# One more expert by seven products, an attention stage moved, and loads in another order: a fused attention and expert kernel

## The chip, the cores and the metric

The kernel runs on one core of a Trainium2 chip. The metric is the device time of one execution in microseconds (us). The kernel before has a median of 362.59 us in 3 runs (362.31 to 362.99). The engines are named as in the profile: PE is TensorE's matmuls, PEld its weight loads, DVE is VectorE, ACT ScalarE, POOL GpSimd and SP SyncE, which mostly issues transfers.

## The reference

Two parts follow each other. The first is attention in blocks: the keys and values of 4 batches of 8 heads (768 positions, 64 wide) are mixed block by block with a matrix that five rounds of exponential and normalisation make from `sort_net`; each of the 8 blocks of queries then attends to one block of 96 mixed keys and values. The second is a mixture of 4 experts on the 3072 resulting rows of 512 values.

```python
k_sorted = np.einsum('bhij,bhjcd->bhicd', P, k_b).reshape(B, H, S, D)
v_sorted = np.einsum('bhij,bhjcd->bhicd', P, v_b).reshape(B, H, S, D)
...
scores = scale * np.matmul(q_b, k_sb.transpose(0, 1, 2, 4, 3))
attn = softmax(scores)                       # written out in the reference
attn_out = np.matmul(attn, v_sb)
...
p = domain_probs / (domain_probs.sum(-1, keepdims=True) + 1e-09)
for e in range(E):                           # x: 3072 x 512, w1[e]: 512 x 1024, w2[e]: 1024 x 512
    h = np.maximum(x @ w1[e], 0.0)
    out += p[:, e:e + 1] * (h @ w2[e])
```

## The kernel before

The rows of a batch are worked on in three chunks of 256. The 12 chunks are numbered g = 0 to 11, and g = 5 (`G0`) is the third chunk of batch 1, counting batches from 0. The attention of a batch is spread in small stages over the expert chunks of earlier batches: each chunk calls `slot()` at fixed places, and a plan says which stages run there. An entry `(2, 0, st_x, 3, 2)` means: chunk 2, slot 0, stage `st_x` for batch 3, pair of heads 2. The program keeps its order on every engine.

The first layer (x times w1) of early chunks is ordinary: for each expert 8 blocks of output, 4 matmuls of 256 columns each, evicted by VectorE from two buffers of PSUM.

```python
def chunk_first(b, c, es, first, slot):
    ...
    for e in es:
        for g in range(2):
            ps = psm([P, 4, 2 * P], F32, ...)
            for f in range(4):
                for kc in range(NKC):                      # NKC = 4
                    nc.tensor.matmul(ps[:, f, :], w1sb[e][:, kc, ...], xT[:, kc, ds(2 * c * P, 2 * P)], ...)
            nc.vector.scalar_tensor_tensor(out=Hb[...], in0=ps[:], scalar=0.0, op0=ALU.max, in1=pb[...], op1=ALU.mult)
            ...                                            # block sums of the expert before
            slot()
```

From G0 on the first layer goes by seven products of half-size blocks in place of eight (a Strassen-like scheme). It needs four sums of weight blocks for each expert (`input_sums`: s1, s3, n2, s4) and four sums of token blocks (`token_sums`). Each product is 8 matmuls of 128 columns. X, Z and Q are PSUM banks of 512 columns; ScalarE copies Z to X so that both go on accumulating:

```python
def seven(g, e):
    ...
    def p1():
        product(Z, "a11", "b11", True)
        nc.scalar.copy(X, Z)
    def p5():
        product(Q, "s1", "t1", True)
    def p6():
        product(X, "n2", "n2")
        nc.scalar.copy(u2, X)
    def p2():
        product(Z, "a12", "b21")
        finish(0, 0, Z)                # VectorE: relu, times the expert's weight
    def p7():
        product(X, "s3", "t3")
        nc.scalar.copy(u3, X)
        tt(t22, Q, u3, ALU.add)
    def p4(): ...                      # X, then finish(1, 0, X)
    def p3(): ...                      # Q, then t12 = Q + u2
```

At G0 expert 0 is still ordinary, and the seven products start with expert 1. `last_banks(n)` closes a PSUM pool, takes four banks (X, Z, two Q) in its place and opens X with one matmul of 512 columns:

```python
def last_chunk(g, slot=None):
    lead = int(g == G0)
    if lead:
        chunk_first(b, c, [0], 0, slot)
        last_banks(0)
        last_tmp(g)
        prs = {1: seven(g, 1)}
        prs[1][1](); prs[1][5](); seven(g, 2)[5](); prs[1][2](); prs[1][6]()
        input_sums(0, 0, True)
        input_sums(0, 1, True)
        last_banks(1)
    else:
        last["e0"][2]()
        prs = {0: last["e0"]}
    ...
    for e in range(1 + lead, E):
        now, prev = prs[e], prs[e - 1]
        now[1]()
        prev[7]()
        ...
        now[2]()
        now[6]()
        prev[22](); prev[4](); prev[3]()
```

In later chunks expert 0's p1 and p5 run in the chunk before, between output products (`last_begin`), and its p6 inside the b22 product. The sums of weight blocks are made ahead. For experts 0 and 1 VectorE adds; for 2 and 3 ScalarE copies a block and a transfer of GpSimd's queue adds to it:

```python
def input_sums(e, n, vector=False):
    ...
    if vector:
        nc.vector.tensor_tensor(a[dst], a[y], a[x], ...)
    else:
        nc.scalar.mul(a[dst], a[x], sign)
        nc.gpsimd.dma_start(a[dst], a[y], accum_op=ALU.add)

PLAN_A = [    # chunk, slot, expert, which sum, on VectorE
    (1, 8, 1, 0, True), (1, 8, 1, 1, True), (1, 8, 1, 2, True), (1, 10, 1, 3, True),
    (1, 8, 2, 0), (1, 8, 2, 1), (1, 9, 3, 0), (1, 10, 3, 1), (1, 11, 2, 2), (1, 12, 3, 2), (1, 13, 2, 3),
    (2, 0, 3, 3),
]
```

The second layer of a chunk is seven products too, of 16 matmuls of 256 columns. The end of the chunk ahead of G0:

```python
    two = [psm([P, 2, 512], F32, ...) for n in range(2)]
    bankA, bankB, bankC, bankQ = [two[n // 2][:, n % 2, 0:DH] for n in range(4)]
    times(bankA, blk(0, 0), "b11", es)
    ...
    times(bankA, blk(0, 1), "t3", es, False)
    tt(ob2, bankA, p5[:], ALU.add)
    tt(ob1, bankA, ob1, ALU.add)
    store(1, ob)
    slot()                                     # slot 13: st_a(3, 2)
    times(bankQ, blk(1, 0), "b22", es, False)
    tt(oa2, bankQ, u2[:], ALU.add)
    slot()                                     # slot 14: st_a(3, 3), the last attention stage
    store(0, oa)
```

`st_a` is probabilities times values: two groups of 8 matmuls into the two buffers of a PSUM pool, each evicted by a reciprocal and a product on VectorE. The end of the last chunk of all:

```python
    product(bankQ, sm(0), "t1")
    nc.scalar.copy(p5[:], bankQ)
    product(bankA, sm(1), "t2", False)
    nc.scalar.copy(u2[:], bankA)
    ...
    product(bankQ, blk(1, 0), "b22", False, range(2))
    product(bankA, blk(0, 1), "t3", False)
    tt(ob2, bankA, p5[:], ALU.add)
    tt(ob1, bankA, ob1, ALU.add)
    nc.sync.dma_start(o[:, 2 * c + 1, :], ob[:])
    product(bankQ, blk(1, 0), "b22", False, range(2, E))
    tt(oa2, bankQ, u2[:], ALU.add)
    nc.sync.dma_start(o[:, 2 * c, DH:Dm], oa2)
```

Early in the program GpSimd issues the loads of batch 1 behind those of six weight matrices of 1 MB:

```python
for qd in range(2):
    for nm in ("v", "k"):
        load_natural(1, nm, qd)
    if qd == 0:
        load_queries(1, range(2))
```

`st_q` transposes a pair of query heads by a transfer of SyncE's queue (slot 7 of chunk 0 for the first pair of batch 1), `st_v` and `st_k` mix values and keys (slots 9 to 11), `st_s` makes scores (slot 0 of chunk 1).

The softmax here doesn't subtract the row's maximum and nothing guards it: scores larger than these inputs give would overflow.

## Time and profile before

| what | value |
|---|---|
| median time | 362.59 us |
| span of the profiled run | 362.4 us |
| instructions | 10776 |
| PE busy | 98% of the span |
| PEld busy | 87% |
| DVE busy | 76% |
| ACT busy | 48% |
| POOL busy | 37% |
| mean transfer rate | 112 GB/s |

Busy times are sums over the whole span; what a single change is worth is read from the stage that it touches. A timeline line gives start and duration in us, then the engine, the source line of the kernel before, the operation, what it writes and reads with partitions and elements, how many instructions are merged, and in brackets how long the engine was idle before and who released it. The duration of a merged group of matmuls includes the modelled run-out of the last one, so that the starts of neighbouring groups are the better measure. A line of the list of waits gives the total in us, how often, and the longest.

### The profile page before, as it was taken

Reading aid. Unit: us, or ns where it says so; the run is one execution under the profiler, and the core shown is the slowest. Engines: PE = TensorE matmul, PEld = TensorE weight load, DVE = VectorE, ACT = ScalarE, POOL = GpSimd, SP = SyncE. Lnnn points to the kernel's source line nnn. Section 1 sums busy time; section 2 is a strip of 40 time slices with the busy share of each in tenths; the row PEclk is TensorE's granted clock in tenths of the full one; section 3 lists DMA queues with packets and bytes.
Section 4 is the critical chain, followed back from the end, with each engine's and each line's share of the span. In section 5 each row is a group of like instructions: output and inputs, shape, how many; then the busy total and the mean of one; then the engine's idle time right before and its main releaser. Section 6 shows DMA issues by size and latency. Waiting matters only on the chain.

```text
span 362.4 us, 10776 instructions
## 1 busy us (share of the span) xinstructions
PE 354.0 (98%) x4589; PEld 315.0 (87%) x4589; DVE 276.8 (76%) x560; ACT 173.6 (48%) x305; POOL 134.1 (37%) x148
## 2 busy tenths in 40 slices
PE   8899999989999999999999999999999999999996
PEld 8785857778888888988889999999999998999995
DVE  5654898769788777868978978867779679587794
ACT  2664330451434355377938257165283481561740
POOL 8872010736022330000626318137055082180470
PEclk9999999999999999999999999999999999999999
DMA  7999999999999999935995210210401201102101
GB/s 99 207 207 231 209 209 202 194 187 194 214 116 142 203 127 173 165 70 69 179 192 88 60 60 2 60 60 3 89 32 50 70 3 58 62 2 63 56 15 46
DMA packets 71676, 40.47 MB, mean 112 GB/s; under 512 B 40518, under 2 KB 66380, under 8 KB 71628
## 3 DMA queue, kind: packets, MB, share of 16 engines
q0 software_dynamic: 36560, 19.93, 41.6%
q1 hardware_dynamic: 35068, 19.85, 27.4%
q8 instruction: 36, 0.59, 0.7%
q14 instruction: 12, 0.10, 0.1%
HBM read 42.00 MB, written 6.34 MB: 133 GB/s over the span
## 4 chain that ended last, share of the span: by engine, by line
PE 75%; DMA 18%; DVE 3%; SPq 1%; ACT 1%; issue 1%; POOL 0%; DVEq 0%; ACTq 0%; POOLq 0%
PE ps_Q L1141 24%; PE ps_h L768 13%; PE ps_p L753 10%; PE ps_X L1038 10%; DMA arena<-in_q_dram 8%; PE ps_Q L1038 7%; PE ps_Z L1038 7%; DMA w<-in_moe_w_dram 6%; DMA vs<-arena 2%; DMA qT<-arena 2%; PE ps_a L441 2%; PE ps_s L406 1%; SPq L368 1%; PE ps_v L354 1%; PE ps_k L387 1%
## 5 line engine op out<-in xcount | busy, mean ns | idle before, releaser
L1051 POOL TENSOR_TENSOR Hb<-tmp,pb 128x512 f16<-128x512 f32 x40 | 50.8, 1277 | 84.3 <-ACT tmp L1050 83.1
L768 PE MATMUL ps_h<-xT,w 128*128 128x256 f16 x576 | 67.8, 273 | 0.0
L768 PEld LDWEIGHTS <-w 128*128 128x128 f16 x576 | 55.1, 98 | 7.4
L774 DVE SCALAR_TENSOR_TENSOR Hb<-ps_h,pb 128x1024 f16<-128x1024 f32 x36 | 44.0, 1223 | 19.8 <-PE ps_h L768 19.6
L1141 PEld LDWEIGHTS <-Hb 128*128 128x128 f16 x560 | 53.4, 98 | 5.6
L1038 PEld LDWEIGHTS <-w 128*128 128x128 f16 x864 | 52.4, 98 | 1.0
L1141 PE MATMUL ps_Q<-w,Hb 128*128 128x256 f16 x336 | 43.4, 273 | 0.0
L1038 PEld LDWEIGHTS <-arena 128*128 128x128 f16 x552 | 33.4, 98 | 0.3 <-issue 0.2
L413 ACT ACTIVATE ET<-ps_s 96x768 f16<-96x768 f32 x24 | 18.1, 802 | 28.4 <-PE ps_s L406 28.1
L121 POOL DMA_DIRECT2D arena<-in_q_dram x24 | 19.9, 836 | 26.9 <-DMA qT<-arena 16.6
L1038 PE MATMUL ps_X<-kT,arena 128*128 128x128 f16 x384 | 29.3, 219 | 0.1
L1074 DVE TENSOR_TENSOR tmp<-ps_Q,tmp 128x512 f32<-128x512 f32 x26 | 18.0, 692 | 14.6 <-ACT tmp L1073 10.4
L1058 ACT COPY ps_X<-ps_Z 128x512 f32<-128x512 f32 x27 | 15.4, 570 | 28.3 <-PE ps_Z L1038 27.9
L396 ACT CAST kT<-ps_k 64x384 f16<-64x384 f32 x48 | 22.7, 473 | 12.8 <-PE ps_k L387 11.8
L739 DVE TENSOR_TENSOR Sb<-Hb 128x512 f16<-128x512 f16 x45 | 26.3, 609 | 0.9 <-POOL Hb L1051 0.8
L1141 PE MATMUL ps_Q<-T,Hb 128*128 128x256 f16 x224 | 26.7, 273 | 0.0
L1050 ACT ACTIVATE tmp<-tmp 128x512 f32<-128x512 f32 x40 | 25.4, 634 | 1.2 <-DVE tmp L1074 1.0
L753 PEld LDWEIGHTS <-Hb 128*128 128x128 f16 x232 | 21.9, 98 | 3.0
L1141 PEld LDWEIGHTS <-Sb 128*128 128x128 f16 x224 | 21.9, 98 | 2.5
L1065 ACT COPY tmp<-ps_X 128x512 f32<-128x512 f32 x26 | 15.2, 586 | 13.2 <-PE ps_X L1038 13.2
L1051 POOL TENSOR_TENSOR Hb<-tmp7x,pb 128x512 f16<-128x512 f32 x14 | 19.0, 1356 | 5.7 <-ACT tmp7x L1050 5.7
L1044 DVE SCALAR_TENSOR_TENSOR Hb<-ps_X,pb 128x512 f16<-128x512 f32 x27 | 18.5, 684 | 2.7 <-PE ps_X L1038 2.7
(205 smaller groups left out, 652.7 us busy)
## 6 DMA issues: line engine op xcount, KB each, us to landing
w<-in_moe_w_dram POOLq DMA_DIRECT2D x7, 1024.0 KB, 27.4
pb<-p_dram SPq DMA_DIRECT2D x12, 512.0 KB, 5.4
arena<-in_k_dram POOLq DMA_DIRECT2D x8, 384.0 KB, 8.8
arena<-in_v_dram POOLq DMA_DIRECT2D x8, 384.0 KB, 8.9
vs<-arena SPq DMA_DIRECT2D x36, 66.0 KB, 5.7
arena<-in_q_dram POOLq DMA_DIRECT2D x24, 96.0 KB, 7.3
out_dram<-ob SPq DMA_DIRECT2D x9, 256.0 KB, 2.0
out_dram<-oa SPq DMA_DIRECT2D x8, 256.0 KB, 2.3
```

What stands on the lines that cost most here:

```text
L121: nc.gpsimd.dma_start(t[:, h // 2, :, h % 2, :], q[b, h].rearrange("(t p) d -> p t d", p=P))
L396: nc.scalar.copy(kT[ds(D * hh, D), r], pk[ds(D * r, D), hh].rearrange("p a (i c) -> p a i c", c=CP),)
L413: nc.scalar.activation(ETs[2 * (pr % 2) + hh][:, 0:S].rearrange("c (a x) -> c a x", a=2), pss[hh][0:BLK, :, 0:HS], AF.Exp, bias=0.0, scale ...
L739: tt(sm[0], blk(0, 1), blk(1, 1), ALU.add)
L753: nc.tensor.matmul(ps, lhs(e, f), Ts[e][rhs][:, f, :], start=(first and e == es[0] and f == 0), stop=(done and e == es[-1] and f == KH - 1 ...
L768: nc.tensor.matmul(ps[:, f, :], w1sb[e][:, kc, ds((4 * g + f) * P, P)], xT[:, kc, ds(2 * c * P, 2 * P)], start=(kc == 0), stop=(kc == NKC ...
L774: nc.vector.scalar_tensor_tensor(out=Hb[:, e, ds(4 * g, 4), :], in0=ps[:], scalar=0.0, op0=ALU.max, in1=pb[:, ds(e, 1), :].broadcast_to([P ...
L1038: nc.tensor.matmul(dst[:, ds(f * P, P)], a[lhs][:, k, ds(f * P, P)], t[rhs][:, k, :], start=(first and f == 0 and k == 0), stop=(f == KH - ...
L1044: nc.vector.scalar_tensor_tensor(out=Hb[:, e, ds(i * KH, KH), ds(j * P, P)], in0=src.rearrange("p (f x) -> p f x", f=KH), scalar=0.0, op0= ...
L1050: nc.scalar.activation(src, src, AF.Relu, bias=0.0, scale=1.0)
L1051: nc.gpsimd.tensor_tensor(Hb[:, e, ds(i * KH, KH), ds(j * P, P)], src.rearrange("p (f x) -> p f x", f=KH), pb[:, ds(e, 1), ds(j * P, P)].b ...
L1141: nc.tensor.matmul(ps, lhs(e, f), Ts[e][rhs][:, f, :], start=(first and e == 0 and f == 0), stop=(e == E - 1 and f == KH - 1), skip_group_ ...
```

## The change

Expert 0 of G0 goes by seven products like the others, so that the ordinary first layer is gone from there on. For this the four sums of its weight blocks are needed a chunk sooner: VectorE makes them at slots 1, 3 and 5 of the second chunk and slot 0 of the third. They take a third block of a buffer that attention results used, and those go to another place. The output products of the second chunk already use the new banks, and expert 0's p1, p5 and p6 start there. The last attention stage moves from slot 14 into the b22 product, between its second and third expert. Two smaller things go with it: the first query heads of batch 1 are loaded ahead of its values and keys, and in the last chunk the t1 and b22 products are made in two halves of 128 columns, so that the output's last quarter is stored in two pieces, on two queues.

```diff
     def st_a(b, pr):
         if b == B - 1 and pr >= H // 2 - 2:
-            xsl = Sflat[:, ds((pr + 4) * NB * 2 * D, NB * 2 * D)]...
+            xsl = arena[:, ds((pr + 2) * NB * 2 * D, NB * 2 * D)]...
@@ PLANS
-            (1, 14, st_a, 3, 3), (2, 0, st_x, 3, 2), (2, 1, st_x, 3, 3),
+            (2, 0, st_x, 3, 2), (2, 1, st_x, 3, 3),
@@ chunk
-        if b or c:
+        if (b, c) == divmod(G0 - 1, R // 2):
+            last_banks(1)
+            bankA, bankB, bankC, bankQ = [last[nm][at][:, 0:DH] for nm, at in (("X", 1), ("Z", 1), ("Q", 2), ("Q", 3))]
+        elif b or c:
...
-            times(bankQ, blk(1, 0), "b22", es, False)
+            if last["X"]:
+                last_tmp(G0, range(1), ())
+                last_begin(G0)
+                def between():
+                    last["e0"][6]()
+                    st_a(B - 1, H // 2 - 1)
+                times(bankQ, blk(1, 0), "b22", es, False, True, between, 2)
+            else:
+                times(bankQ, blk(1, 0), "b22", es, False)
@@ last_banks: banks by name, in reverse order for n = 1; the opening matmul apart
+        for nm, at in [("X", n), ("Z", n), ("Q", 2 * n), ("Q", 2 * n + 1)][:: -1 if n else 1]:
+            last[nm][at] = pool.tile([P, 512], F32, ...)
+    def written(n):
         nc.tensor.matmul(last["X"][n][:], w1sb[0][:, 0, 0:P], w1sb[0][:, 1, 0:512], start=True, stop=True)
@@ last_begin
+        if g == G0:
+            e0[1](lambda: (e0[5](), written(1)))       # p5 and the opener between p1 and its copy
@@ last_chunk
+        last["e0"][2]()
         if lead:
-            chunk_first(b, c, [0], 0, slot)
+            last["e0"][7]()
+            slot()
             last_banks(0)
-            ...                                        # the special start with expert 1, two input_sums
-            last_banks(1)
+            written(0)
+            slot()
+            last_tmp(g, range(1, 2))
+        prs = [last["e0"]] + [seven(g, e) for e in range(1, E)]
+        for e in range(1, E):
             now[1]()
-            prev[7]()
+            if e > 1 or not lead:
+                prev[7]()
...
+            now[5]()
             now[2]()
             now[6]()
...
+        ends = [(bankQ, ds(0, P), nc.scalar), (bankB, ds(P, P), nc.sync)] if final else [(bankQ, ds(0, DH), nc.sync)]
+        for bank, part, _ in ends:
+            product(bank[:, part], sm(0), "t1", part=part)
+            nc.scalar.copy(p5[:, part], bank[:, part])
...
+        early = 1 if final else 2                      # experts of b22 ahead of t3
...
+        for bank, part, queue in ends:
+            product(bank[:, part], blk(1, 0), "b22", False, range(early, E), ..., part)
+            tt(oa2[:, part], bank[:, part], u2[:, part], ALU.add)
+            if final:
+                queue.dma_start(o[:, 2 * c, DH:Dm][:, part], oa2[:, part])
@@ PLAN_A
+        (1, 1, 0, 0, True), (1, 3, 0, 1, True), (1, 5, 0, 2, True), (2, 0, 0, 3, True),
@@ loads
+    load_queries(1, range(2))
     for qd in range(2):
         for nm in ("v", "k"):
             load_natural(1, nm, qd)
-        if qd == 0:
-            load_queries(1, range(2))
```

Cuts are marked with `...` and `@@`. The order of blocks for the weight sums (`A_ORDER`) changes in one entry, from 3 to 14, and the sums of G0 that VectorE made between output products are gone with the start that needed them.

## The prediction

> **What bounds the kernel now.** I read first the busy shares of the page, then who waited for whom, then the chain of waits, and last the timelines of single engines around the places that the change touches.
>
> ```profile
> PE 354.0 (98%) x4589; PEld 315.0 (87%) x4589; DVE 276.8 (76%) x560; ACT 173.6 (48%) x305; POOL 134.1 (37%) x148
> PE ps_s L406 <- DMA qT<-arena: 1.9, 1, 1.9
> ```
>
> TensorE is busy for 354.0 of 362.4 us, so a change can gain only by taking matmul time away or by filling one of the few holes. The second line, from the list of waits, names the largest hole after the start: scores wait once, 1.9 us, for transposed queries. The chain of waits says where that comes from, and the timelines of GpSimd and TensorE and the list of DMA landings (last columns: KB, us from issue to landing) give the times:
>
> ```profile
> 16.76 23.39 DMA w<-in_moe_w_dram
> 40.44 27.25 DMA arena<-in_q_dram
> 67.75 6.01 DMA qT<-arena
> ...
> 27.66 0.81 POOL L110 DMA_DIRECT2D arena<-in_v_dram  x1 [0.66 <-PE ps_mv L483]
> 28.46 0.75 POOL L110 DMA_DIRECT2D arena<-in_k_dram  x1
> ...
> arena<-in_v_dram POOLq DMA_DIRECT2D x1, 384.0 KB, 34.9
> arena<-in_k_dram POOLq DMA_DIRECT2D x1, 384.0 KB, 36.1
> ...
> 65.18 0.49 PE L354 MATMUL ps_v<-arena 128*128 128x384 f16 x2
> 68.45 0.50 PE L387 MATMUL ps_k<-arena 128*128 128x128 f16 x6
> 73.89 0.52 PE L406 MATMUL ps_s<-qT,kT 64*128 64x96 f16 x16 [1.89 <-DMA qT<-arena]
> ```
>
> The values (V) of batch 1 land at 27.66 + 34.9 = 62.6 us, the keys (K) at 28.46 + 36.1 = 64.6, the second head of queries at 40.44 + 27.25 = 67.7; only then can the transpose start, which takes 6.0 us, and the scores run at 73.9 instead of 72.0. V, by contrast, is used at 65.2 and K at 68.5, so they have slack.
>
> The other place is the start of batch 1's third chunk (timelines of TensorE and of ScalarE):
>
> ```profile
> 181.82 1.91 PE L753 MATMUL ps_p<-w,Hb 128*128 128x256 f16 x16
> 183.56 0.94 PE L441 MATMUL ps_a<-vs,ET 96*128 96x65 f16 x16
> 184.34 3.66 PE L768 MATMUL ps_h<-xT,w 128*128 128x256 f16 x32
> 187.83 0.38 PE L1004 MATMUL ps_X<-w 128*128 128x512 f16 x1
> ...
> 182.08 1.99 ACT L968 ACTIVATE w<-w 128x1024 f16<-128x1024 f16 x2
> ```
>
> Starts are more reliable than durations here: the 32 matmuls of expert 0 take 187.83 - 184.34 = 3.49 us. The last attention stage takes 184.34 - 183.56 = 0.78 us instead of the 0.48 that the same stage takes at 176.80 to 177.28: 0.3 us of waiting for VectorE to free its banks. And the last line shows two copies on ScalarE, some 0.95 us apart, which at present run beside expert 0's matmuls, when nobody needs ScalarE.
>
> [...] groups of 8 matmuls of 128 columns start 0.447 us apart (234.26, 234.71), 55.8 ns each; groups of 16 of 256 columns 1.747 us apart, 109.2 ns each. [...] the landings of this trace do come in the order of issue (62.6, 64.6, then q at 65.2 and 67.7). [...]
>
> **The change part by part.**
>
> 1. Queries of batch 1 before K and V. The queue is a line that is full until 71 us, so bytes do not come sooner in sum, only in another order. The two query heads took 67.7 - 64.6 = 3.1 us of it, K 2.0, V about 1.9, and the weights ahead of them end at 62.6 - 1.9 = 60.7. New order: queries at 60.7 + 3.1 = 63.8, V at 65.7, K at 67.7. The transpose then starts at 63.8 and lands at 69.8, before 72.0: the hole of 1.89 us closes. But V now lands at 65.7, and its matmul stood at 65.18: a new hole of about 0.6 us including the signal. K (67.7) is still ahead of 68.45 + 0.6. Net -1.9 + 0.6 = **-1.25 us**. From 74 us on TensorE is nearly gapless and its transfers are triggered by its own progress, so I expect this to reach the end.
>
> 2. Expert 0 by seven products. 32 x 109.2 ns = 3.49 us go; 7 x 8 = 56 matmuls x 55.8 ns = 3.12 us come: -0.37 us.
>
> 3. Last attention stage inside the b22 product. The bank wait of 0.3 us goes, since first-layer products now lie between the two attention stages. The present third chunk also shows gaps of 0.22, 0.15, 0.09 and 0.09 us (191.17, 191.76, 193.18, 195.05), because expert 1 began without a product to hide ScalarE's copies behind. Gone in the steady pattern: together -0.3 - 0.55 = -0.85 us. So parts 2 and 3 would bring -1.2.
>
> 4. What this part brings in. Follow ScalarE in the new order, on the old clock up to the t3 product (179.57). TensorE: t3 to 181.32, attention 181.80, expert 0's p1 and p5 182.70, the 512-column bank opener 182.92, half of b22 183.79, p6 184.24, attention 184.72, rest of b22 185.60, p2 186.05, p7 186.50, second opener 186.72, expert 1's p1 and p5 187.62; next is expert 1's p2, which needs ScalarE's copy of Z to X. ScalarE's copy of p7's result starts 0.70 us after p7's first matmul (as at 209.53 and 210.23), at 186.75. Behind it in program order now stands the 0.95 us copy of a weight block for expert 3's fourth sum (slot 0 of this chunk), until 188.3. Only then comes the copy Z to X, and TensorE goes on 0.63 us after its start (as 210.23 to 210.86): 188.9. That is a **new hole of 1.3 us**. From p2 of expert 1 to the next chunk's p1 the steady chunk takes 234.26 - 213.53 = 20.73 us, so the next chunk would begin at 209.65 against 209.53: **+0.1 us**. The gain of parts 2 and 3 is given back.
>
> 5. Block sums of expert 0 on VectorE a chunk sooner: four operations of 0.68 us move from the third chunk into slots 1, 3 and 5 of the second and slot 0 of the third. In VectorE's timeline it stands idle for 0.85, 0.52 and 0.75 us ahead of the evictions that follow these slots (157.30, 161.68, 166.05); such an operation takes 0.6 us from start to start. One eviction comes 0.1 us later, which two buffers hide. **0 us**.
>
> 6. Halves at the end of the last chunk. The t1 and b22 products of 256 columns become two of 128: 32 pairs x (2 x 55.8 - 109.2) = +0.08 us. The last add falls from 0.42 to about 0.28, like other VectorE work of half the size; the last store is 64 KB instead of 128, the other half and the big store of ob are under way earlier:
>
> ```profile
> 357.93 1.04 PE L1141 MATMUL ps_Q<-w,Hb 128*128 128x256 f16 x8
> 358.97 0.33 SPq L1193 DMA_DIRECT2D out_dram<-ob  x1
> 359.07 0.42 DVE L1197 TENSOR_TENSOR oa<-ps_Q,u 128x256 f32<-128x256 f32 x1
> 359.53 0.33 SPq L1199 DMA_DIRECT2D out_dram<-oa  x1
> ```
>
> Only half an expert's worth of b22 stays ahead of t3, so ob is stored at about 358.6, and the last store goes out at 359.45; its bytes need not queue behind 256 KB any more (384 KB took some 1.3 us of DMA at 300 to 400 GB/s). I take **-0.4 us**.
>
> Sum: -1.25 + 0.1 + 0 - 0.4 = -1.55. 362.6 - 1.6 = **361.0 us**.
>
> **Rivals.** (a) ScalarE's weight copy does not stand in the way, or stands elsewhere in the order: then the third chunk gains its 1.2 us and the time is about 359.7. For it: the change is plainly built to smooth this start. Against: the slot is called between p7 and expert 1's p1, and the engine keeps its order. (b) The new bank assignment in the second chunk makes the first output product wait for the last eviction of the first layer: that one runs from 168.13 to 169.36, while the product starts at 168.26, so +1.1 us, about 362.1. Against: the banks are taken in reverse, so that the first two products get the buffer that was evicted first (by my count of the pool's tiles). (c) V is later than I work out, or the transpose is held up by the loads beside it: the DMA line is only moved and the hole reappears under another name, 362.2. For it: in this trace a transpose takes from 2.8 to 9.4 us. (d) V's wait is smaller, because query transfers in small pieces overlap with V's: 360.5.
>
> **Range and chances.** The independent spreads are about 0.6 us for part 1, 0.8 for parts 2 to 4 (mostly downwards, rival a) and 0.2 for the end: 359.6 to 362.1 should hold it 8 times in 10. Two per cent are 7.25 us; the holes left on TensorE after the start do not sum to that, so "faster" gets 0.01; "slower" would need several new waits in series: 0.02.
>
> **What would show it.** Part 1: no wait of the scores (L406 before) for qT, the query DMA landing near 64, and a wait of the first V matmul of about 0.6 us near 65. Part 4: ScalarE's copy w<-w directly before its copy ps_X<-ps_Z early in the third chunk, and a gap of TensorE of about 1.3 us there; if there is none, the third chunk is right by rival a. Parts 2 and 3: 56 more matmuls of 128 columns and 32 fewer of 256; no stretched last attention stage. Part 6: last store issued within 0.1 us of the matmuls' old place, and a shorter rest behind it. A wait of L753 near 167 would prove rival b. If the scores still wait for qT, part 1 was wrong.

## The result, and the profile after

| | median, us | executions | ratio to before, 95% interval |
|---|---|---|---|
| before | 363.13 (362.31 to 363.94) | 6 | |
| changed | 364.81 (364.06 to 365.83) | 6 | 1.0048 [1.0027, 1.0068] |
| changed, measured again with the last experiments | 364.55 (before there: 363.60) | 22 | 1.0028 [1.0011, 1.0044] |

The change costs 1.0 to 1.7 us; it was predicted to bring 1.55, and 361.0 us with a top of 362.1 was too low. The profiled execution of the changed kernel took 365.83 us (its span in the trace is 364.0 us), 1.0 above the median; that of the kernel before, 364.18 us, is as far above its own. So a single wait of this trace may belong to one execution, and the experiments below are also used to see which waits come back.

First the page of the changed kernel, its line of busy times:

```profile
PE 352.9 (97%) x4645; PEld 314.8 (86%) x4645; DVE 278.8 (77%) x563; ACT 176.3 (48%) x311; POOL 136.7 (38%) x150
```

TensorE has 56 instructions more and 1.1 us less of busy time. The time grew all the same, so it went into holes. The list of waits of TensorE names them (us in total, times, longest); waits that both kernels have before 15 us, of ps_R, ps_w and two of 0.2 us, are left out:

```profile
PE ps_Z L1050 <- ACT ps_X L1072: 1.0, 1, 1.0
PE ps_X L753 <- DVE Hb L774: 1.0, 1, 1.0
PE ps_a L441 <- DMA vs<-arena: 1.0, 1, 1.0
PE ps_a L441 <- ACT arena L981: 0.8, 1, 0.8
PE ps_mv L483 <- DMA arena<-in_v_dram: 0.6, 1, 0.6
PE ps_s L406 <- DMA qT<-arena: 0.3, 1, 0.3
```

The scores' wait for queries fell from 1.9 to 0.3 us, but five other waits stand in its place. Two come of the change itself. The first is at the start of the second chunk's output products (timeline of VectorE and TensorE; start, duration, instruction, in brackets the idle time before it and who ended it):

```profile
165.98 1.23 DVE L774 SCALAR_TENSOR_TENSOR Hb<-ps_h,pb 128x1024 f16<-128x1024 f32 x1
...
168.06 1.23 DVE L774 SCALAR_TENSOR_TENSOR Hb<-ps_h,pb 128x1024 f16<-128x1024 f32 x1 [0.86 <-PE ps_h L768]
...
169.34 1.91 PE L753 MATMUL ps_X<-w,Hb 128*128 128x256 f16 x16 [0.98 <-DVE Hb L774]
```

These are the last two evictions of the first layer. The product starts at 169.34, when the *last* one ends. In the kernel before (same view) it starts 0.13 us after the last eviction has begun:

```profile
168.13 1.23 DVE L774 SCALAR_TENSOR_TENSOR Hb<-ps_h,pb 128x1024 f16<-128x1024 f32 x1 [0.86 <-PE ps_h L768]
168.26 1.91 PE L753 MATMUL ps_p<-w,Hb 128*128 128x256 f16 x16
```

The second is expert 1's start in the third chunk (timeline of ScalarE and TensorE of the changed kernel):

```profile
188.50 0.58 ACT L1087 COPY tmp<-ps_X 128x512 f32<-128x512 f32 x1 [1.61 <-PE ps_X L1050]
...
188.98 0.61 PE L1050 MATMUL ps_Q<-kT,arena 128*128 128x128 f16 x8
188.98 1.06 ACT L981 ACTIVATE w<-w 128x1024 f16<-128x1024 f16 x1
189.94 0.59 ACT L1072 COPY ps_X<-ps_Z 128x512 f32<-128x512 f32 x1
190.58 0.61 PE L1050 MATMUL ps_Z<-xT,w 128*128 128x128 f16 x8 [0.99 <-ACT ps_X L1072]
```

p7's copy, then the weight block, then the copy Z to X, then TensorE: the order that the prediction worked out, with a hole of 0.99 us where it gave 1.3.

The loads (timeline of SyncE and TensorE, changed kernel):

```profile
62.20 2.25 SPq L375 DMA_TRANSPOSE qT<-arena  x1
...
65.78 0.49 PE L354 MATMUL ps_v<-arena 128*128 128x384 f16 x2
...
72.90 0.52 PE L406 MATMUL ps_s<-qT,kT 64*128 64x96 f16 x16 [0.30 <-DMA qT<-arena]
```

and how long the transposing load and the last load in the line took (views of qT and of the transfers issued near 50.70 us, where that load is issued; last column us to landing):

```profile
DMA to landing us min/median/max: 10.6/10.6/10.6
```

```profile
arena<-in_k_dram POOLq DMA_DIRECT2D x1, 384.0 KB, 21.6
```

The transpose is issued 5.5 us sooner than before (62.20, not 67.75), but lands only 1.0 us sooner: 62.2 + 10.6 = 72.8 against 67.75 + 6.01 = 73.8. The last load, K of the second half of batch 1, lands at 50.7 + 21.6 = 72.3. What stands ahead of the transpose in its own queue is taken up below.

The end (timeline of the last matmuls, adds and stores, changed kernel):

```profile
359.52 1.50 PE L1149 MATMUL ps_Q<-w,Hb 128*128 128x128 f16 x24
...
360.78 0.37 ACTq L1207 DMA_DIRECT2D out_dram<-oa  x1
361.06 0.29 DVE L1205 TENSOR_TENSOR oa<-ps_Q,u 128x128 f32<-128x128 f32 x1 [0.31 <-PE ps_Q L1149]
361.38 0.33 SPq L1207 DMA_DIRECT2D out_dram<-oa  x1
```

From the start of the last group of matmuls to the span's end are 364.0 - 359.52 = 4.48 us, of which 24 matmuls take 24 x 55.8 ns = 1.34; before, 362.4 - 357.93 = 4.47, of which 8 matmuls take 0.87. The rest behind the matmuls is 3.14 instead of 3.60 us; with the 0.08 us of matmuls more, -0.38. That is the tail alone; ahead of it the t3 product came to wait for its bank (ScalarE and TensorE, changed kernel):

```profile
357.15 0.61 PE L1149 MATMUL ps_Q<-w,Hb 128*128 128x128 f16 x8
357.35 0.37 ACT L1185 COPY u<-ps_Q 128x256 f32<-128x256 f32 x1 [1.48 <-PE ps_Q L1149]
357.77 1.91 PE L1149 MATMUL ps_Q<-T,Hb 128*128 128x256 f16 x16
```

The copy to u2 empties the bank that t3 accumulates in next. The 8 short matmuls between take 8 x 55.8 ns = 0.45 us, t3 starts 0.62 us after the first of them, 0.05 after the copy ends: a hole of 0.18 us (0.176 to 0.179 in nine executions with the halves, e4 aside, none in those without). Before, 8 matmuls of 256 columns (0.87 us) covered the copy.

### The profile page after: what moved, and what is told of

Its sections match the earlier page's. It is cut to its first block, busy times and chain, and to the rows that moved or that the text cites. A ratio compares the mean times of both kernels' runs of the same rounds, so it can differ in the third digit from the quotient of the medians.

```text
span 364.0 us, 10905 instructions
## 1 busy us (share of the span) xinstructions
PE 352.9 (97%) x4645; PEld 314.8 (86%) x4645; DVE 278.8 (77%) x563; ACT 176.3 (48%) x311; POOL 136.7 (38%) x150
## 3 DMA queue, kind: packets, MB, share of 16 engines
q1 hardware_dynamic: 35068, 19.79, 28.5%
## 5 line engine op out<-in xcount | busy, mean ns | idle before, releaser
L1063 POOL TENSOR_TENSOR Hb<-tmp,pb 128x512 f16<-128x512 f32 x42 | 53.4, 1279 | 83.4 <-ACT tmp L1062 82.1
L768 PE MATMUL ps_h<-xT,w 128*128 128x256 f16 x544 | 64.2, 273 | 0.0
L768 PEld LDWEIGHTS <-w 128*128 128x128 f16 x544 | 52.0, 98 | 7.0
L1050 PEld LDWEIGHTS <-w 128*128 128x128 f16 x896 | 54.2, 98 | 1.8 <-issue 1.1
L774 DVE SCALAR_TENSOR_TENSOR Hb<-ps_h,pb 128x1024 f16<-128x1024 f32 x34 | 41.5, 1224 | 16.4 <-PE ps_h L768 15.9
L1149 PE MATMUL ps_Q<-w,Hb 128*128 128x256 f16 (+1 forms) x352 | 43.4, 268 | 0.0
L1050 PEld LDWEIGHTS <-arena 128*128 128x128 f16 x504 | 30.2, 98 | 0.0
L1088 DVE TENSOR_TENSOR tmp<-ps_Q,tmp 128x512 f32<-128x512 f32 x27 | 18.7, 692 | 14.8 <-ACT tmp L1087 10.6
L1062 ACT ACTIVATE tmp<-tmp 128x512 f32<-128x512 f32 x42 | 26.6, 634 | 2.3 <-DVE tmp L1088 1.3
L739 DVE TENSOR_TENSOR Sb<-Hb 128x512 f16<-128x512 f16 x45 | 27.6, 638 | 0.0
L1050 PE MATMUL ps_X<-kT,arena 128*128 128x128 f16 x336 | 25.6, 219 | 0.0
L753 PEld LDWEIGHTS <-Hb 128*128 128x128 f16 x232 | 21.9, 98 | 4.2 <-issue 1.1
```

The costliest lines, as they stand in the source:

```text
L739: tt(sm[0], blk(0, 1), blk(1, 1), ALU.add)
L753: nc.tensor.matmul(ps, lhs(e, f), Ts[e][rhs][:, f, :], start=(first and e == es[0] and f == 0), stop=(done and e == es[-1] and f == KH - 1 ...
L768: nc.tensor.matmul(ps[:, f, :], w1sb[e][:, kc, ds((4 * g + f) * P, P)], xT[:, kc, ds(2 * c * P, 2 * P)], start=(kc == 0), stop=(kc == NKC ...
L774: nc.vector.scalar_tensor_tensor(out=Hb[:, e, ds(4 * g, 4), :], in0=ps[:], scalar=0.0, op0=ALU.max, in1=pb[:, ds(e, 1), :].broadcast_to([P ...
L1050: nc.tensor.matmul(dst[:, ds(f * P, P)], a[lhs][:, k, ds(f * P, P)], t[rhs][:, k, :], start=(first and f == 0 and k == 0), stop=(f == KH - ...
L1062: nc.scalar.activation(src, src, AF.Relu, bias=0.0, scale=1.0)
```

## The experiments

The theory after the result: the 1.06 us of the bank wait and two wrong sizes in the loads explain the loss; the hole at expert 1's start is a second cost, which cancels the gains of the third chunk. The rival: the loss lies in the loads or in ScalarE's turns, and the bank wait only renames idle time. All runs are timed in 5 rounds against the kernel before on the same chip, but for the last (one execution).

| run | what it is | median, us (before there) | ratio, 95% interval |
|---|---|---|---|
| e1_loads | before, with the loads' order alone | 363.92 (363.21) | 1.0018 [1.0004, 1.0033] |
| e2_ends | before, with the end in halves alone | 363.30 (363.21) | 0.9999 [0.9980, 1.0018] |
| e3_third | before, with the third chunk alone | 364.67 (363.21) | 1.0043 [1.0027, 1.0060] |
| e4_nopool | changed, banks from first-layer tiles | 406.53 (363.21) | 1.1203 [1.1184, 1.1222] |
| e5_copymove | changed, weight turn after the copy | 363.38 (363.16) | 1.0004 [0.9993, 1.0016] |
| e6_twopool | changed, two pools | 363.46 (363.16) | 1.0009 [0.9997, 1.0021] |
| e7_v7 | changed, V stage one slot sooner | 364.54 (363.16) | 1.0042 [1.0024, 1.0059] |
| e8_late | before, queries first, later V and K | 369.64 (363.16) | 1.0183 [1.0160, 1.0206] |
| e9_both | changed, e5 and e6 together | 363.00 (363.60) | 0.9981 [0.9958, 1.0004] |
| e10_both_oldloads | e9 with the old order of loads | 363.23 (363.60) | 0.9988 [0.9968, 1.0008] |
| e11_after_again | changed | 364.55 (363.60) | 1.0028 [1.0011, 1.0044] |
| e12_unrev | changed, banks in plain order | 363.44, one execution | |

**e1_loads.** The kernel before with this edit alone:

```diff
+    load_queries(1, range(2))
     for qd in range(2):
         for nm in ("v", "k"):
             load_natural(1, nm, qd)
-        if qd == 0:
-            load_queries(1, range(2))
```

> Only the loads of batch 1 in the new order, on the kernel before. The trace of the changed kernel shows two things: the wait of the scores for transposed queries shrinks from 1.9 to 0.3 us, and later, near 124 us, the values times probabilities of batch 2 wait 1.0 us for the transfers vs<-arena, where before it was 0.3. Theory A (transfers are nearly full up to there, so the lead is eaten at the next wait for a transfer): 0.5 to 0.8 us faster than before, with the wait for vs near 124 us again about 1 us. Rival B (the wait for vs was chance in one execution): 1.4 to 1.6 us faster, and no wait for vs above 0.4 us.

Measured: 0.2 % slower, 0.65 us by the ratio. Both theories missed. The list of waits and the view of qT of this run:

```profile
PE ps_s L406 <- DMA qT<-arena: 1.5, 1, 1.5
```

```profile
L375 SPq DMA_TRANSPOSE qT<-arena x1: 2103/2103/2103, 61.5 to 61.5; - x1
...
DMA to landing us min/median/max: 11.8/11.8/11.8
```

Issued at 61.5 and landed at 73.3: the transposing load goes out early and is hardly sooner there. That is what the prediction's rival (c) expected; what held the transpose up is worked out further below. Why the kernel gets slower rather than staying level isn't seen in this trace.

**e2_ends.** The kernel before with the last t1 and b22 products in two halves and three stores:

```diff
-        product(bankQ, blk(1, 0), "b22", False, range(2, E), ...)
-        tt(oa2, bankQ, u2[:], ALU.add)
-            nc.sync.dma_start(o[:, 2 * c, DH:Dm], oa2)
+        for bank, part, queue in ends:                 # [(bankQ, first 128, ACT's queue), (bankB, last 128, SP's)]
+            product(bank[:, part], blk(1, 0), "b22", False, range(early, E), ..., part)
+            tt(oa2[:, part], bank[:, part], u2[:, part], ALU.add)
+            queue.dma_start(o[:, 2 * c, DH:Dm][:, part], oa2[:, part])
```

> Only the two halves at the end of the last chunk, on the kernel before. Theory A (the tail is shortened as in the changed kernel's trace: last store 0.25 us earlier against its own chunk, matmuls 0.08 longer): 0.2 to 0.3 us faster. Rival B (the smaller rows of the two stores cost what the shorter add brings): within 0.1 us of before.

Measured: level, with an interval of -0.7 to +0.7 us. The traces give -0.38 at the tail and +0.18 ahead of it, -0.2 in all, which lies inside; the times alone can't show it.

**e3_third.** The kernel before with everything of the change that touches chunks two and three (seven products, banks by name, the attention stage inside b22, the sums on VectorE), old loads and old end.

> Only the rebuilt third chunk of batch 1, with loads and end as before. Theory A (its three new waits, 1.0 us of the first output product for VectorE, 0.8 us of the attention stage, 1.0 us of expert 1's p2 for ScalarE, outweigh the 1.2 us that seven products and the fuller pattern save): 1.2 to 2.2 us slower than before, all of it gained between 165 and 191 us. Rival B (the loss lies in the loads or at the end): within 0.3 us of before.

Measured: +0.43 %, about 1.5 us (interval 1.0 to 2.2), as much as the whole change loses. Its list of waits has the two that come of the change:

```profile
PE ps_Z L1050 <- ACT ps_X L1072: 1.0, 1, 1.0
PE ps_X L753 <- DVE Hb L774: 1.0, 1, 1.0
```

The wait of 0.8 us for the attention stage near 183 us isn't there.

**e4_nopool.** The bank wait alone, without closing the pool: the last stage's four banks are halves of two ordinary two-bank tiles of the first layer's pool, which stays open.

```diff
-            last_banks(1)
+            two = [psm([P, 2, 512], F32, f"ps_p{n}_{b}_{c}") for n in range(2)]
+            for n, (nm, at) in enumerate((("X", 1), ("Z", 1), ("Q", 2), ("Q", 3))):
+                last[nm][at] = two[n // 2][:, n % 2, :]
```

> The changed kernel, but the four banks of the second chunk are taken as two more tiles of the first layer's pool in place of closing that pool. Theory A (closing a pool makes the first user wait for the last reader of any of its tiles, whichever banks it gets): the wait of the first output product for the eviction, 1.0 us, is gone, and st_v behind it comes 1 us sooner, so that the attention stage finds its values landed: 1.6 to 2.0 us faster than the changed kernel. Rival B (the eviction itself is what the product needs, as it reads Hb): the wait stays and the time is within 0.3 us of the changed kernel. Rival C (the bank wait goes but the attention stage goes on waiting, for ScalarE's copy of a weight block): 1.0 us faster, and a wait of 0.8 to 1.8 us at the attention stage.

Measured: 12 % slower, which none of the theories had. The list of waits of this run:

```profile
PE ps_p L1052 <- DVE Hb L1058: 16.9, 21, 1.2
PE ps_p L1052 <- DVE tmp L1090: 9.3, 6, 1.6
PE ps_p L1151 <- ACT ob L1179: 2.3, 5, 0.5
```

The wait at L753 is gone, but 43 us are lost, 28.5 of them in these 32 waits of products for readers of their tile. All that the edit does to these chunks is that X and Z, and the two Q, are halves of one tile, so a dependence in this run goes by tile and not by bank. As a test of the bank wait the run is worth little, since the pairs changed too; e6 leaves them apart.

**e5_copymove.** The hole of expert 1 alone: the turn of the last weight block moves behind p6's copy.

```diff
                 def between():
                     last["e0"][6]()
+                    input_sums(3, 3)
                     st_a(B - 1, H // 2 - 1)
@@ PLAN_A
-        (2, 0, 3, 3),
```

> The changed kernel, with one thing moved: the turn of the first weight tile of the last block sum (w<-w on ScalarE, 1.06 us, which in the changed kernel stands between the two evictions of expert 1's start) is taken behind the copy that lets expert 1's next product begin. Theory A (the copy is late because ScalarE works in order and the turn is ahead of it): the wait of ps_Z for the copy, 1.0 us in the changed kernel, goes to 0.1 or less, and the time falls by 0.8 to 1.1 us against the changed kernel, to about +0.2 % over the kernel before. Theory B (the copy waits for its own eviction or for the bank, and the turn only fills a gap): the wait stays over 0.7 us and the time within 0.2 us of the changed kernel.

Measured: theory A. Timeline of ScalarE and TensorE of this run:

```profile
185.76 1.06 ACT L982 ACTIVATE w<-w 128x1024 f16<-128x1024 f16 x1
...
187.47 0.58 ACT L1088 COPY tmp<-ps_X 128x512 f32<-128x512 f32 x1 [0.66 <-PE ps_X L1051]
...
188.16 0.57 ACT L1073 COPY ps_X<-ps_Z 128x512 f32<-128x512 f32 x1
...
188.78 0.61 PE L1051 MATMUL ps_Z<-xT,w 128*128 128x128 f16 x8 [0.21 <-ACT ps_X L1073]
```

The turn now lies in time that ScalarE had free, the two copies follow each other, and 0.21 us of the 0.99 are left. So ScalarE's order was the cause: in the changed kernel the copy Z to X starts 0.96 us after the turn ahead of it (189.94 and 188.98), here 0.69 us after p7's copy (188.16 and 187.47). That the engine keeps the program's order was a premise of the prediction; these two runs show it at this place. The time is level with the kernel before (+0.15 us by the ratio), which is 0.9 us below the changed kernel as e11 timed it and 1.6 below its first timing.

**e6_twopool.** The bank wait alone: the first layer's two tiles come from two pools, closed one by one, and the last stage's four banks stay four tiles.

```diff
-        (openA, openM)[n].close()
-        pool = ctx.enter_context(tc.tile_pool(name=f"ps7_{n}", bufs=1, ...))
-        for nm, at in [("X", n), ("Z", n), ("Q", 2 * n), ("Q", 2 * n + 1)][:: -1 if n else 1]:
-            last[nm][at] = pool.tile(...)
+        names = [("X", n), ("Z", n), ("Q", 2 * n), ("Q", 2 * n + 1)]
+        for op in (openM1, openM0) if n else (openA,):
+            op.close()
+        for i, part in enumerate([names[:1:-1], names[1::-1]] if n else [names]):
+            pool = ctx.enter_context(tc.tile_pool(name=f"ps7_{n}_{i}", bufs=1, ...))
+            for nm, at in part:
+                last[nm][at] = pool.tile(...)
```

> The changed kernel, with the first layer's two accumulators in two pools of one buffer each, closed one after the other, so that the bank of expert 0's first output product is bound to the eviction that read that bank and not to the last one. All four tiles of the last stage stay separate. Theory A (the wait of 1.0 us at L753 comes of closing one pool for both accumulators): the wait of ps_X for DVE at L753 goes, the attention transposes that queue behind it on TensorE start 1 us sooner, and the wait of 0.8 us of the last attention stage goes with it: 1.0 to 1.9 us faster than the changed kernel, that is equal to or up to 0.2 us faster than the kernel before. Theory B (the product would have to wait for something else at the same place): another wait of 0.7 us or more stands there, and the time is within 0.3 us of the changed kernel.

Measured: theory A. Timeline of this run:

```profile
167.06 1.22 DVE L784 SCALAR_TENSOR_TENSOR Hb<-ps_h,pb 128x1024 f16<-128x1024 f32 x1 [0.85 <-PE ps_h L778]
167.20 1.91 PE L763 MATMUL ps_X<-w,Hb 128*128 128x256 f16 x16
```

The product again starts 0.14 us after the last eviction has begun, as in the kernel before. The bank was free all the time; what the product waited for was the release of the pool. The time is +0.3 us by the ratio, 0.7 us below e11 and 1.4 below the first timing. The 0.8 us near 183, which theory A counted in, was no part of it (see e7).

**e7_v7.** The wait near 183 us was put down to ScalarE's weight turn at L981. V's stage was moved ahead of the waiting product instead, since V's last transfer landed at 175.8 + 7.1 = 182.9 us:

```diff
-            (1, 6, st_k, 3, 2), (1, 7, st_k, 3, 3), (1, 8, st_v, 3, 3), ...
+            (1, 6, st_k, 3, 2), (1, 7, st_k, 3, 3), (1, 7, st_v, 3, 3), ...
```

> The changed kernel, with the last V stage of batch 1's third chunk run one slot sooner, ahead of the product that waits for its bank, so that its DMA is issued about 1 us sooner. Theory A (the attention stage near 183 us waits for V, which landed at 182.9 since its issue stood behind the bank wait): the 0.8 us wait of that stage goes to 0.2 or less, the bank wait at L753 falls from 1.0 to about 0.6 since the moved work (four transposes) fills part of it; 0.5 to 1.2 us faster than the changed kernel. Theory B (the wait is what it is put down to, ScalarE's weight copy at L981): the 0.8 us stays and the time moves by less than 0.4 us.

Measured: 0.3 us below the changed kernel, not separable from nothing. The bank wait fell to 0.47 us (timeline):

```profile
168.35 1.91 PE L753 MATMUL ps_X<-w,Hb 128*128 128x256 f16 x16 [0.47 <-DVE Hb L774]
```

The attention stage doesn't wait here, but neither does it in e3, e5, e6, e9, e11 and e12, where V's stage stands in its old place. So the 0.8 us belong to the one execution shown above, and this run can't tell what caused them.

**e8_late.** The kernel before, queries first, and V and K of batch 1's second half loaded from inside the stages, so that less is in the line beside the transpose:

```diff
-            ..., (0, 11, st_k, 1, 0), (0, 11, st_n, 1, 1),
-            (1, 0, st_q, 1, 1), (1, 0, st_s, 1, 0), (1, 0, st_n, 1, 2), ...
+            ..., (0, 11, st_k, 1, 0), (0, 11, st_lv, 1, 1), (0, 11, st_n, 1, 1),
+            (1, 0, st_q, 1, 1), (1, 0, st_s, 1, 0), (1, 0, st_lk, 1, 1), (1, 0, st_n, 1, 2), ...
@@ loads
-    for qd in range(2):
-        for nm in ("v", "k"):
-            load_natural(1, nm, qd)
-        if qd == 0:
-            load_queries(1, range(2))
+    load_queries(1, range(2))
+    for nm in ("v", "k"):
+        load_natural(1, nm, 0)
```

> The kernel before, with batch 1's queries loaded first and V and K of its second half issued later, inside the stages, so that the queue has little in it when the transposing load of the queries is issued. Theory A (the transposing load takes 10 to 12 us only because it shares the queues with the loads ahead of it): it takes 6 to 7 us, the scores' wait for qT of 1.5 us goes, and the time is 1.0 to 1.9 us below the kernel before, unless the later V or K make a new wait. Theory B (it takes its 10 us whatever is beside it): the wait stays at 1 us or more and the time is within 0.4 us of before.

Measured: 1.8 % slower, and theory A on its point (view of qT):

```profile
L375 SPq DMA_TRANSPOSE qT<-arena x1: 1992/1992/1992, 62.3 to 62.3; - x1
...
DMA to landing us min/median/max: 5.8/5.8/5.8
```

Issued at 62.3 us, as in the changed kernel, the transpose takes 5.8 us instead of 10.6, and the scores don't wait. The time is lost later: the loads put off push the transposes and loads behind them, a load of pb (the experts' weights of a chunk's tokens, 512 KB) is issued at 92.05 instead of 85.65 us and lands at 92.05 + 8.7 = 100.75, too late for an eviction, and TensorE stands still for 3.5 of the 6.6 us lost; where the rest goes isn't followed here (timeline):

```profile
100.80 2.36 DVE L774 SCALAR_TENSOR_TENSOR Hb<-ps_h,pb 128x1024 f16<-128x1024 f32 x2 [5.07 <-DMA pb<-p_dram]
102.08 6.51 PE L768 MATMUL ps_h<-xT,w 128*128 128x256 f16 x32 [3.50 <-DVE Hb L774]
```

**e9_both.** The edits of e5 and e6 together.

> The changed kernel with both mends: two pools for the first layer's accumulators, and the turn of the last weight tile taken behind the copy. Theory A (the two waits are separate costs of the third chunk and both stand on TensorE's path): no wait of 0.5 us or more on TensorE between 160 and 200 us, and the gains of the two single mends (1.4 us each against the changed kernel) add up to 2 to 2.8 us: 0.3 to 1.1 us faster than the kernel before, ratio 0.997 to 0.999. Theory B (they overlap: mending one lets the other take up the time): not more than 1.6 us faster than the changed kernel, so level with the kernel before.

Measured: theory A on the waits, but not on the gain: 363.00 against 364.55 us for the changed kernel beside it, 1.55 us, which theory B allowed. The first product and expert 1's p2 (timeline):

```profile
167.49 1.91 PE L763 MATMUL ps_X<-w,Hb 128*128 128x256 f16 x16
...
187.23 0.61 PE L1066 MATMUL ps_Z<-xT,w 128*128 128x128 f16 x8 [0.21 <-ACT ps_X L1088]
```

On TensorE the two costs are separate and add up: from the attention stage near 124 us to p1 of the next chunk (the first table below) the changed kernel e11 takes 85.51 us, e5 84.81, e6 84.63 and e9 83.85, so 0.70 + 0.88 = 1.58 us singly and 1.66 together. What didn't add up are the single gains as timed, 1.4 us each by medians taken at another time; they were larger than the waits removed. Against the kernel before, the interval [0.9958, 1.0004] includes no difference: e9 mends the change, and isn't shown to beat what was there.

**e10_both_oldloads.** e9 with the loads in the old order (the edit of e1 the other way).

> As the run with both mends, but with batch 1's starting loads in the order of the kernel before. Theory A (the new order of the loads gives nothing or costs a little, as the order alone did with +0.18 %): 0 to 0.7 us faster than the run with both mends, and the fastest of all; the scores' wait for qT of 1.5 to 1.9 us comes back. Theory B (the new order is worth what its wait shows once nothing else is in the way): 0.7 to 1.6 us slower than the run with both mends.

Measured: level with e9 (363.23 and 363.00): neither a gain nor the 0.7 us and more of theory B is seen, and with intervals of some 0.8 us to either side nothing smaller can be told. The scores don't wait in this execution of the old order.

**e11_after_again.** The changed kernel unchanged.

> The changed kernel unchanged, beside the mended ones on the same chip: 1.3 to 2.1 us above the kernel before, with the bank wait of 1.0 us at L753 and the wait of 1.0 us of ps_Z for the copy. Whether the attention stage near 183 us waits again for V tells if that wait belongs to the kernel (then 0.6 to 0.9 us) or to the one execution shown (then 0.2 or less).

Measured: +0.28 %, 1.0 us, less than the 1.3 expected at least. Its timeline has two waits between 60 and 200 us:

```profile
167.72 1.91 PE L753 MATMUL ps_X<-w,Hb 128*128 128x256 f16 x16 [0.98 <-DVE Hb L774]
...
188.05 0.61 PE L1050 MATMUL ps_Z<-xT,w 128*128 128x128 f16 x8 [0.99 <-ACT ps_X L1072]
```

Neither the 0.8 us near 183 nor the 1.0 us for V near 124 us come back. What belongs to the changed kernel are these two.

**e12_unrev.** The banks of the last stage in plain order:

```diff
-        for nm, at in [("X", n), ("Z", n), ("Q", 2 * n), ("Q", 2 * n + 1)][:: -1 if n else 1]:
+        for nm, at in [("X", n), ("Z", n), ("Q", 2 * n), ("Q", 2 * n + 1)]:
```

> The changed kernel with the banks of its last stage taken in plain order and not in reverse. Theory A (what the first product waits for is the closing of the pool, so the last reader of any of its banks): the same wait of 0.9 to 1.1 us at L753, wherever its bank lies. Theory B (it waits for the readers of its own bank): in plain order its bank is one of those that the last eviction reads, in reverse it is not, and the waits of the two orders differ by the 1 us between the two evictions.

Measured: theory A (timeline):

```profile
167.89 1.91 PE L753 MATMUL ps_X<-w,Hb 128*128 128x256 f16 x16 [0.98 <-DVE Hb L774]
```

In either order 0.98 us, the last eviction's end. The order of the banks has no part in it.

## Why the prediction was wrong

The runs give two tables. The first has the times between four points that don't depend on how the start of an execution went: the attention stage near 124 us, the first output product of the second chunk, p1 of the next chunk (209.53 us before), and the end of the span.

| trace | near 124 to first product, us | first product to p1, us | p1 to the end, us |
|---|---|---|---|
| before | 43.28 | 41.27 | 152.87 |
| changed | 44.42 (wait of 0.98) | 41.99 (hole 0.99, attention 0.75) | 152.67 |
| changed, e11 | 44.43 (0.98) | 41.08 (0.99) | 152.70 |
| e5, turn moved | 44.51 (0.98) | 40.30 (0.21) | 152.68 |
| e6, two pools | 43.37 | 41.26 (0.99) | 153.04 |
| e9, both | 43.37 | 40.48 (0.21) | 152.93 |

In the last column e6 and e9 have a further hole of 0.28 us near 344 us, whose cause isn't known; e7 and e10 have it too.

The second follows the transposing load: when TensorE began V of batch 1, when pb was issued to SyncE's queue ahead of the transpose and landed, when the transpose was issued, moved its first packet and landed, when the last load issued before it landed (K of the second half), and the scores.

| trace | order | V | pb issued, landed | transpose issued, first packet, landed | last load landed | scores (wait) |
|---|---|---|---|---|---|---|
| before | old | 65.18 | 61.13, 69.5 | 67.75, 69.44, 73.8 | 71.4 | 73.89 (1.89) |
| e2 | old | 66.94 | 62.89, 72.9 | 67.23, 68.52, 74.7 | 73.1 | 74.83 (1.07) |
| e3 | old | 68.78 | 64.73, 72.0 | 66.50, 68.13, 72.9 | 71.5 | 75.54 (none) |
| e10 | old | 65.87 | 61.82, 71.6 | 65.67, 68.53, 72.5 | 71.6 | 72.63 (none) |
| changed | new | 65.78 | 61.72, 71.5 | 62.20, 68.67, 72.8 | 72.3 | 72.90 (0.30) |
| e1 | new | 65.10 | 61.04, 69.7 | 61.52, 68.31, 73.3 | 72.7 | 73.46 (1.53) |
| e11 | new | 65.42 | 61.37, 70.8 | 61.85, 67.75, 72.2 | 71.7 | 72.30 (none) |
| e9 | new | 66.41 | 62.35, 71.2 | 62.83, 67.83, 73.1 | 72.5 | 73.25 (none) |

**Part 1, -1.25 us: wrong, about 0 in its place.** The step that failed is "The transpose then starts at 63.8 and lands at 69.8". It took the 6.0 us of the kernel before for a time that holds in any place, and it left SyncE's own queue out. In the new order the transpose is issued even sooner, at 61.5 to 62.8, but 0.48 us behind pb, a load of 512 KB in the same queue. What the queues moved in the 6.4 us after the issue (timeline of SyncE, and the view of the transfers from 62.2 to 68.6 us, changed kernel; packets and MB, q1 is SyncE's queue, q0 GpSimd's):

```profile
61.72 0.38 SPq L213 DMA_DIRECT2D pb<-p_dram  x1
62.20 2.25 SPq L375 DMA_TRANSPOSE qT<-arena  x1
...
q0 software_dynamic: 1302, 0.97, 98.7%
q1 hardware_dynamic: 452, 0.46, 25.9%
```

By the packet records of the trace the 452 packets of q1 have 1 KB each, as pb's 512 have, of which the first begins at 65.34 us; the transpose moves 768 packets of 256 bytes, of which the first begins at 68.67 and the last ends at 72.14. In the kernel before they run from 69.44 to 72.86. In all eight executions of the table the first packet begins between 67.7 and 69.5 us, whether the transpose was issued at 61.5 or at 67.8: the 5.5 us of lead go by while pb waits and is moved. V and K act through pb: with their second half put off (e8) pb, still directly ahead, takes 5.5 us instead of 9.7, and the packets of the transpose run from 64.51 to 67.68. So rival (c), "the transpose is held up by the loads beside it", is half the mechanism. No run issues the transpose ahead of pb, so that the queue's order is what costs the lead is read from the packets and not tested.

The transpose thus lands at 72.2 to 73.3 us in place of 72.5 to 74.7. The wait of 1.89 us also was no fixed cost: two of the table's four executions of the old order have none, and scores without a wait follow V by some 6.8 us, where V itself began anywhere between 65.1 and 68.8. Alone the order measured +0.65 us (interval 0.15 to 1.2), in e9 against e10 -0.2, within the spread; no gain is seen in either. V's new wait of 0.6 us didn't come: V landed at 35.15 + 28.5 = 63.7, two microseconds before the 65.7 worked out.

**Parts 2 to 4, +0.1: right, -0.2 measured.** From the first product to the next chunk's p1 the changed kernel takes 41.08 us (e11) against 41.27. The new hole came where and for the reason predicted, with 0.99 instead of 1.3 us, and moving the turn (e5) gives back 41.08 - 40.30 = 0.78 of it. Rival (a), 359.7 us, fell. That the sum came out a little better than +0.1 is luck: where the first product comes late, the scores stage near 174 us takes 0.45 us, where it comes in time 0.63 (six executions each), so 0.18 of the -0.19 hang on the bank wait; with two pools (e6) the stretch takes 41.26 us, -0.01.

**The bank of the first product, 0 in the sum: wrong, +1.06.** This is the step that turns the sign. Rival (b) had it with +1.1 us and was set aside with "Against: the banks are taken in reverse, so that the first two products get the buffer that was evicted first". The bank was indeed free. But the banks come from a pool that is opened where the first layer's pool closes, and that close waited here for the last reader of either of its tiles. Both orders wait 0.98 us (e12), two pools none (e6), and the stretch before the first product is 44.43 us with the wait and 43.37 without: 1.06 us, or 0.88 with the 0.18 that the later scores stage gives back. The count of the tiles answered the wrong question.

**Part 5, 0: right.** The only long wait for VectorE after the start is the one of the eviction at L753, and it goes with two pools while the four sums stay where they are (e6).

**Part 6, -0.4: right at the tail, -0.2 in all.** The tail is 0.38 us shorter, but the prediction saw that less of b22 stays ahead of t3 and didn't ask what it had covered: the hole of 0.18 us ahead of t3 takes half of the gain. The times (e2) neither show nor exclude what is left.

With these in place of the old terms the sum is 0 + 1.06 - 0.19 - 0.20 = +0.7 us. Counted directly, from the attention stage near 124 us to the end, e11 takes 238.21 us and the kernel before 237.42: +0.8. Measured are +1.0 beside e11 and +1.7 the first time, with intervals from 0.4 to 2.5. A remainder of 0.2 to 1.0 us isn't placed. The candidates are seen but not shown: the loads alone measured +0.65 us without a wait in the trace to carry it, and waits for V's transfers of up to 1 us come and go between executions (0.97 us near 124 us in the changed kernel, 0.27 in e12, 0.54 in e10 with the old loads, none in e5, e9 and e11).

## What to carry to other kernels

A buffer taken from a pool that opens where another closes waited here for the last reader of everything in the closed pool, not for the reader of its own memory (0.98 us in either order of the banks, none with two pools): before a rival is dismissed by counting banks, ask what the release is bound to, and give tiles that must come free at different times pools of their own. A transfer's duration read off a trace held only for its place in the line (the transpose took 6.0 us before, 10.6 in the changed kernel, 5.8 in e8): before moving it, look at what stands ahead of it in the queue that issues it and at what shares the engines with it. Work that is thinned out between two uses of a bank may have covered a copy (a hole of 0.18 us ahead of t3 here). And a wait seen in one execution is a sum to be had only if other executions have it too (the 1.89 us of the scores were 1.07, none and none in the three others with the old loads).

## What the runs showed of the hardware

A transposing load of SyncE's queue, issued 0.48 us behind a load of 512 KB of that queue, moved its first packet 5.0 to 6.8 us after its issue (the table's four executions of the new order) and 2.2 us in e8, where less was under way beside it; in the kernel before, 6.6 us behind the same load, 1.7 us. From the first packet to the end of the last were 3.2 to 4.8 us in all eight executions of the table and in e8. In the new order it landed 0.5 to 0.7 us after the last load of GpSimd's queue. How the transfer engines share between the two queues wasn't tried.

A wait is perhaps put down to the wrong engine. The 0.75 us before the attention stage in the changed kernel's trace carry ScalarE's name (timeline):

```profile
183.14 0.64 PE L441 MATMUL ps_a<-vs,ET 96*128 96x65 f16 x16 [0.75 <-ACT arena L981]
```

The same stage's V landed at 182.9 us, 0.2 us ahead of it, and ScalarE's copy at L981 writes a weight block that the stage doesn't read. In e11 V landed at 174.0 + 5.7 = 179.7 us, before the stage's turn, and there was no wait. That V's transfer and not the copy was waited for is inferred from these times; no run tests it.
